# A Fourier mixer ahead of a feed-forward layer: units B multiply over 128 rows, with Y regrouped by SBUF-to-SBUF transfers

## The chip, the cores and the metric

The kernel runs on one core of a Trainium2 chip. The metric is the device time of one execution in microseconds (us), the lower the better. A core has five engines with a queue each: PE (the matrix engine; PEld is its loading of stationary operands), DVE (vector), ACT (activation), POOL (GpSimd) and SP, which in this kernel issues nearly all transfers.

## The reference

For each of 8 batches of 3008 positions by 256 channels, a Fourier transform is taken along the positions, each frequency is multiplied by a complex 256 by 256 matrix, soft-thresholded, and transformed back. All 24064 rows then go through a feed-forward layer with 2048 hidden channels.

```python
X = np.fft.rfft(x, axis=1)
Yr = Xr @ w_r - Xi @ w_i + b_r
Yi = Xr @ w_i + Xi @ w_r + b_i
Y  = sign(Y) * max(|Y| - 0.01, 0)            # Yr and Yi apart
y  = np.fft.irfft(Y, n=3008, axis=1)
h  = y.reshape(24064, 256) @ w_in
g  = where(h > 0, h, exp(min(h, 0)) - 1)
out = g @ w_out
```

## The kernel before

**The transform is cut into small units.** 3008 is 47 times 64, so each transform is made in two stages of matrix products with twiddle factors in the stationary operands. Per batch there are 6 units A (first stage, from the input tiles `xt0` to `xt2`, result to DRAM `DA`), 8 units X (second stage, from `Z`, which is loaded back from `DA`), 12 units M (the complex product, threshold and bias; two make one tile `Y` of 128 rows, 2 frequencies, 512 columns: real part in columns 0 to 255, imaginary part in 256 to 511), 6 units B (first stage back, result `Bz` to DRAM `DB`), and 8 units Y (second stage back, from `Bs`, loaded from `DB`; result `yT`).

**A unit B** (`unit_B`) takes one tile `Y` and multiplies it by `M3`. The rows of `Y` hold two groups `s` of 64 rows. The inverse stage sums over the 64 rows of a group and over the two parts `c`; so for each `(pp, s)` two matmuls of 64 rows are accumulated, one for each `c`. A unit is 8 matmuls of 64 rows by 256 columns, in pairs `s` = 0, 1 that lie on the lower and the upper 64 rows of the matrix engine. Its result of 1024 columns is moved to `Bz` by ACT, or by DVE in steps marked "act"; after every second unit SP stores `Bz` to `DB`. After B5, `load_Bs` brings everything back as `Bs` for the units Y.

**The feed-forward layer runs in 376 steps, 47 per batch.** A step handles 512 rows and 256 hidden channels: `front` makes 4 matmuls into `hps` and the exponential on ACT, `finish_elu` makes `gT` on DVE, and `back`, two steps later (`LAG`), makes 8 matmuls with `w_out_r` into `ps_o`. Every 8 steps `ps_o` is copied to `osb`, which has two buffers, and SP stores it to `out`.

**The order is written out by hand.** `plan(b)` lists for the 47 steps of batch b which unit of the next batch goes ahead of `front` (list `f0`) and what is issued behind it (list `f1`). A step is thus on PE: a unit, 4 matmuls `hps`, 8 matmuls `ps_o`. In steps marked "act" the elu is made by ACT and DVE without POOL, in steps marked "pool" by POOL too. Units M use POOL for three operations each (L301, L302, L303), the last of which writes `Y`. Each queue is in order, and a queue whose head waits holds all that is behind it.

**Tiles.** Pools with a tag have a fixed number of buffers. `Y` has 3 (`wk3`), `XS` (sums of the two parts for the units M) is a tile of its own, `M3` lies in the constant pool. Batch 0 has its own route (`split_B`, `turn_B`), which uses `M3` and `Y` directly; so the unit B of the change is used for batches 1 to 7, 42 times.

Of the kernel before, what the change touches and what calls it, by code (L numbers as in the profile page):

```python
# [8 lines left out]
ALU = mybir.AluOpType  # L9
# [11 lines left out]
N2 = 64  # L21
# [8 lines left out]
def kernel(  # L30
# [25 lines left out]
    constp = ctx.enter_context(tc.tile_pool(name="constp", bufs=1))  # L56
    M1 = constp.tile([P, P], F32R, name="M1")
    M2 = constp.tile([2 * NR, NS, 2, 2 * K1], BF16, name="M2")
    M3 = constp.tile([P, K1 // 2, 2, P], BF16, name="M3")
    M4 = constp.tile([4 * K1, 2 * N1], BF16, name="M4")  # L60
    wcat_r = constp.tile([P, 2, 2 * D], BF16, name="wcat_r")
    wcat_s = constp.tile([P, 2, 2 * D], BF16, name="wcat_s")
    w_in_s = constp.tile([P, 2, DFF], BF16, name="w_in_s")
    w_out_r = constp.tile([P, NFT, E], F32R, name="w_out_r")
    bias_bc = constp.tile([P, 2 * D], F32, name="bias_bc")
    bias_p = constp.tile([P, 2 * D], BF16, name="bias_p")
# [10 lines left out]
    space = constp.tile([P, 384], BF16, name="space")  # L77
# [24 lines left out]
    Z_of = {}  # L102
    XT_of = {}
    Y_of = {}
    Bz_of = {}
    DB_of = {}
    Bs_of = {}
# [119 lines left out]

    def sum_of(dt, ch):

        return XS[:, 3 * dt + ch] if 3 * dt + ch < 5 else busy[:]  # L230

    def three_weights(c, dt):

# [6 lines left out]
    def m_group(b, q, i, ps, biased=False):  # L240
        XT = XT_of[b]
        o = (2 * q + i) * P
        todo = [(c, dt) for c in range(2) for dt in range(2)]
        if b == 0:
            todo.sort(key=lambda z: z[1])
        for c, dt in todo:
            nc.tensor.matmul(  # L247
                ps, lhsT=XT[:, dt, c, o : o + P], rhs=(wcat_r, wcat_s)[c][:, dt, :],
                start=(not biased and (c, dt) == (0, 0)), stop=((c, dt) == (1, 1)),
            )  # L250
        if i == 0:
            Y_of[b, q] = wk3.tile([P, 2, 2 * D], BF16, name="Y", tag="Y")
        if biased:
            yb = ps
        else:
            yb = wk3.tile([P, 2 * D], F32, name="yb", tag="yb")[:]
            nc.vector.tensor_tensor(yb, ps, bias_bc[:], ALU.add)
        if (b, q, i) == (0, 2, 0):
            clip = late3.tile([P, 2 * D], F32, name="gT", tag="gT")
        else:  # L260
            clip = wk2.tile([P, 2 * D], F32, name="clip", tag="clip")
        return yb, clip

    def unit_M(b, q, i):
# [6 lines left out]
            return  # L271
        XT, o = XT_of[b], (2 * q + i) * P
        if i == 0:
            Y_of[b, q] = wk3.tile([P, 2, 2 * D], BF16, name="Y", tag="Y")
# [59 lines left out]
    def last_M(q, i):  # L334
# [26 lines left out]
        for Y_, yb, ch in todo:  # L361
            nc.vector.scalar_tensor_tensor(Y_, yb, LAM, ch, ALU.add, ALU.min)

    def unit_B(b, v, alone=False, on_dve=False, all_dve=False):
        if (b, v // 2) not in Bz_of:
            t = "A" if alone and v == 0 else "Bz"
            Bz_of[b, v // 2] = wk2.tile([P, 8, D], BF16, name=t, tag=t)
            if b not in DB_of:
                DB_of[b] = dram.tile([K1, P, D], BF16, name="DB", tag="DB")
        Bz, Y = Bz_of[b, v // 2], Y_of.pop((b, v))  # L370
        ps = unit_ps("bps", alone)
        for pp in range(2):
            for c in range(2):
                for s in range(2):
                    nc.tensor.matmul(  # L375
                        ps[:, s, pp * D : pp * D + D],
                        lhsT=M3[s * N2 : s * N2 + N2, 2 * v + pp, c, :],
                        rhs=Y[s * N2 : s * N2 + N2, pp, c * D : c * D + D],
                        start=(c == 0), stop=(c == 1),
                    )  # L380
        o = 4 * (v % 2)
        Bv = Bz[:, o : o + 4, :].rearrange("p (q s) d -> p s q d", s=2)
        psv = ps[:].rearrange("p s (q d) -> p s q d", d=D)
        if on_dve:
            nc.scalar.copy(Bv[:, :, 0], psv[:, :, 0])
            nc.vector.tensor_copy(Bv[:, :, 1], psv[:, :, 1])
        else:
            evac(Bv, psv, all_dve)
        if alone:
            k0 = 4 * v  # L390
            nc.sync.dma_start(
                DB_of[b][k0 : k0 + 4].rearrange("k p d -> p k d"), Bz[:, o : o + 4, :]
            )
        elif b == 1 and v > 3:
            nc.sync.dma_start(
                DB_of[b][4 * v : 4 * v + 4].rearrange("k p d -> p k d"), Bz[:, o : o + 4, :]
            )
        elif v % 2:
            k0 = 8 * (v // 2)
            nc.sync.dma_start(DB_of[b][k0 : k0 + 8].rearrange("k p d -> p k d"), Bz[:])  # L400
# [13 lines left out]
    def split_B(v, ps, on_dve=(False, True), by_half=False):  # L414
# [8 lines left out]
        def half(pp):  # L423
            for c in range(2):
                for s in range(2):
                    nc.tensor.matmul(
                        ps[s][:, pp * D : pp * D + D],
                        lhsT=M3[s * N2 : s * N2 + N2, 2 * v + pp, c, :],
                        rhs=Y[s * N2 : s * N2 + N2, pp, c * D : c * D + D],
                        start=(c == 0), stop=(c == 1),  # L430
                    )
# [22 lines left out]
    def turn_B(v, ts=(0, 1), ps=None, on_dve=False):  # L454
# [11 lines left out]
        for pp in range(2):  # L466
            for dt in ts:
                for c in range(2):
                    for s in range(2):
# [7 lines left out]
                            rhs=M3[s * N2 : s * N2 + N2, 2 * v + pp, c, :].rearrange(  # L477
                                "p (g m) -> p g m", g=4
                            )[:, :, 0:8],
                            start=(c == 0), stop=(c == 1),  # L480
# [69 lines left out]
    def idle_pe(n):  # L550

        for _ in range(n):
            nc.tensor.matmul(ips[:], lhsT=busy[:, 0:P], rhs=busy[:], start=True, stop=True)

    nc.vector.memset(bias_p[:], 0.0)
    bpd = dram.tile([3, 2 * D], BF16, name="bpd", tag="bpd")
    idle_pe(9)
# [272 lines left out]
    XS = sump.tile([P, 5, 512], BF16, name="XS")  # L830
# [60 lines left out]
    for o, src, sc, bi in ((1, w3, TURN, 0.0), (0, a3, -TURN, hpi[:])):  # L891
        if o == 0:
            nc.scalar.activation(a3[:], w3[:], AF.Abs)
        nc.scalar.activation(
            M3[:, :, 0, o * N2 : o * N2 + N2], src[:], AF.Sin, bias=bi, scale=sc
        )
    sgb = sg3[:].unsqueeze(2).to_broadcast([P, K1 // 2, N2])
    first_M(3, 0, True)
    nc.vector.scalar_tensor_tensor(
        M3[:, :, 1, 0:N2], M3[:, :, 0, N2:P], 2.0, sgb, ALU.mult, ALU.mult  # L900
    )
    nc.vector.scalar_tensor_tensor(
        M3[:, :, 1, N2:P], M3[:, :, 0, 0:N2], -2.0, sgb, ALU.mult, ALU.mult
    )
    first_M(3, 1, True)
    let_go()
# [203 lines left out]
    def plan(b):  # L1110
# [3 lines left out]
        mode = [None] * PER  # L1114
        n1, n2 = b + 1, b + 2
        mid = [("X", u) for u in range(8)] + [
# [4 lines left out]
        ]  # L1121
        if n1 < B:
            if b:
                lead, xs = 0, (3, 6, 9) if b < 3 else (3, 8, 13)

                def M(q):
                    return [("M", q, 0), ("M", q, 1)]
# [1 line left out]
                shift = b - 1 if b < 3 else b - 3  # L1129
                seq = [("y", 2), ("y", 3)] + [None] * shift + [("X", u) for u in range(8)]  # L1130
                if b < 3:
                    seq += [("y", 4)] + M(0) + M(1) + [("y", 5), ("B", 0)]
                else:
                    seq += M(0) + [("y", 4)] + M(1) + [("y", 5), ("B", 0)]
                seq += M(2) + [("y", 6), ("B", 1)] + M(3) + [("y", 7), ("B", 2)]
                on_act = [("X", 4), ("X", 7), ("B", 3)] + [("y", u) for u in range(5, 8)]
                if b < 3:
                    on_act += [("A", 0)]
                    seq += M(4) + [("B", 3)] + M(5) + [("A", 0), ("B", 4), ("B", 5)]
                    seq += [("A", u) for u in range(1, 6)]  # L1140
# [12 lines left out]
        else:  # L1153
            lead, seq = 0, [("y", u) for u in range(2, 8)]
        for t, u in enumerate(seq, lead):
# [26 lines left out]
        if b == 0:  # L1182
# [106 lines left out]
```

## Time and profile before

| | |
|---|---|
| runs without the profiler, median of 3 | 893.58 us (893.39 to 893.68) |
| span of the profiled execution, first to last instruction | 903.9 us |
| granted PE clock over the span | 0.948 |
| PE busy | 891.3 us, 99% of the span, 6917 matmuls |
| PEld / DVE / ACT / POOL busy | 675.2 / 679.6 / 722.4 / 596.7 us |
| matmuls of the units B (L375) | 336, in 42 units |
| transfers | 105.85 MB, mean 117 GB/s |

The span is the profiled execution's own time: nothing of the program lies around it in the page, and no other time of that execution is given. It is 10.3 us (1.2%) above the median of the runs without profiler. Busy times are unions of the instructions' intervals. A matmul's interval includes the time in which its result passes through the array, so matmuls that follow each other overlap; what one of them costs PE is read from the distance between two starts.

### The profile page before, as it was taken

Reading aid. Unit: us, or ns where it says so; the run is one execution under the profiler, and the core shown is the slowest. Engines: PE = TensorE matmul, PEld = TensorE weight load, DVE = VectorE, ACT = ScalarE, POOL = GpSimd, SP = SyncE. Lnnn points to the kernel's source line nnn. Section 1 sums busy time; section 2 is a strip of 40 time slices with the busy share of each in tenths; the row PEclk is TensorE's granted clock in tenths of the full one; section 3 lists DMA queues with packets and bytes.
Section 4 is the critical chain, followed back from the end, with each engine's and each line's share of the span. In section 5 each row is a group of like instructions: output and inputs, shape, how many; then the busy total and the mean of one; then the engine's idle time right before and its main releaser. Section 6 shows DMA issues by size and latency. Waiting matters only on the chain.

```text
span 903.9 us, 18292 instructions
## 1 busy us (share of the span) xinstructions
PE 891.3 (99%) x6917; PEld 675.2 (75%) x6917; DVE 679.6 (75%) x969; ACT 722.4 (80%) x1001; POOL 596.7 (66%) x806
## 2 busy tenths in 40 slices
PE   9999999999999999999999999999999999999997
PEld 3467667877788777877778777787777877777776
DVE  7788778688866887668866788677876678778776
ACT  6778778888978889798887988878887798776654
POOL 7562550788657886588756877559875697753664
PEclk9999999999999999999999999999999999999998
DMA  8996226631474115632265231643218201241111
GB/s 262 310 258 188 70 71 181 169 119 47 118 209 124 65 50 152 173 117 88 72 181 136 86 116 48 189 140 101 87 53 229 70 24 48 69 108 36 28 44 47
DMA packets 90718, 105.85 MB, mean 117 GB/s; under 512 B 5395, under 2 KB 81174, under 8 KB 87302
## 3 DMA queue, kind: packets, MB, share of 16 engines
q1 hardware_dynamic: 84278, 76.64, 30.0%
q0 software_dynamic: 5968, 27.26, 9.4%
q8 instruction: 54, 0.88, 0.4%
q10 hardware_dynamic: 384, 0.79, 0.3%
q14 instruction: 34, 0.28, 0.1%
HBM read 54.86 MB, written 49.81 MB: 116 GB/s over the span
## 4 chain that ended last, share of the span: by engine, by line
PE 90%; DVE 3%; DMA 3%; ACT 2%; POOL 1%; issue 1%; SPq 0%; DVEq 0%; ACTq 0%; POOLq 0%
PE ps_o L1080 37%; PE hps L1006 36%; PE mps L289 5%; PE bps L375 2%; PE xps L207 2%; PE yps L538 2%; PE aps L170 2%; DVE gT L1048 2%; PE mps L247 1%; DVE Bz L144 1%; DMA xt<-in_x_dram 1%; DMA Z<-DA 1%; DMA DB<-Bz 1%; PE sps L1006 1%; DMA DA<-A 0%
## 5 line engine op out<-in xcount | busy, mean ns | idle before, releaser
L1048 DVE SCALAR_TENSOR_TENSOR gT<-Et,hps 128x512 fp32r<-128x512 f32 (+1 forms) x544 | 423.7, 811 | 158.5 <-POOL Et L1059 115.4
L1080 PE MATMUL ps_o<-w_out_r,gT 128*128 128x256 f32 x3008 | 481.4, 303 | 0.0
L1080 PEld LDWEIGHTS ps_o<-w_out_r,gT 128*128 128x128 f32 x3008 | 407.7, 190 | 52.4 <-ACT osb L1092 0.5
L1059 POOL TENSOR_SCALAR Et<-Et 128x512 f32<-128x512 f32 x434 | 258.3, 614 | 223.6 <-ACT Et L1022 213.2
L1006 PE MATMUL hps<-yT,w_in_s 128*128 128x512 bf16 (+7 forms) x1688 | 388.9, 360 | 2.0 <-DVE gT L1048 1.3
L1022 ACT ACTIVATE Et<-hps 128x512 f32<-128x512 f32 x412 | 224.2, 598 | 67.8 <-PE hps L1006 63.3
L1006 PEld LDWEIGHTS <-w_in_s 128*128 128x128 bf16 x1728 | 144.7, 99 | 119.7 <-issue 21.7
L1024 ACT ACTIVATE Et<-hps 128x1024 f32<-128x1024 f32 x130 | 133.6, 1027 | 57.3 <-PE hps L1006 49.0
L1025 ACT ACTIVATE Et<-Et 128x1024 f32<-128x1024 f32 x130 | 137.4, 1057 | 4.1
L301 POOL TENSOR_TENSOR yb<-yb,bias_bc 128x512 f32<-128x512 f32 x72 | 92.3, 1282 | 9.5 <-DVE yb L296 9.4
L303 POOL TENSOR_TENSOR Y<-yb,clip 128x512 bf16<-128x512 f32 x72 | 92.6, 1286 | 6.0
L296 DVE TENSOR_TENSOR yb<-mps,yb 128x512 f32<-128x512 f32 x72 | 49.8, 692 | 7.6 <-PE hps L1006 0.5
L146 ACT CAST XT<-xps 128x768 bf16<-128x768 f32 x57 | 45.5, 799 | 9.8 <-PE xps L207 9.7
L146 ACT CAST A<-aps 128x1024 bf16<-128x1024 f32 x40 | 40.5, 1014 | 11.4 <-PE aps L170 9.9
L302 POOL TENSOR_SCALAR clip<-yb 128x512 f32<-128x512 f32 x72 | 44.2, 614 | 6.3
L289 PE MATMUL mps<-wcat_s,XT 128*128 128x256 bf16 x288 | 44.1, 277 | 0.0
L144 DVE COPY yb<-mps 128x256 f32<-128x256 f32 x72 | 30.3, 421 | 11.1 <-PE mps L289 9.7
L1050 DVE SCALAR_TENSOR_TENSOR gT<-hps,Et 128x1024 fp32r<-128x1024 f32 x29 | 35.5, 1223 | 2.4
L224 POOL TENSOR_TENSOR XS<-XT 128x512 bf16<-128x512 bf16 x30 | 34.1, 1159 | 2.1 <-ACT XT L146 1.2
L1092 DVE COPY osb<-ps_o 128x512 f32<-128x512 f32 x46 | 31.6, 686 | 1.2 <-PE ps_o L1080 0.5
L146 ACT CAST Bz<-bps 128x1024 bf16<-128x1024 f32 x32 | 31.9, 998 | 0.5 <-PE bps L375 0.4
L1027 ACT ACTIVATE Et<-hps 128x1024 f32<-128x1024 f32 x29 | 29.8, 1029 | 2.6 <-PE hps L1006 1.2
(184 smaller groups left out, 678.8 us busy)
## 6 DMA issues: line engine op xcount, KB each, us to landing
xt<-in_x_dram POOLq DMA_DIRECT2D x21, 1024.0 KB, 5.4
out_dram<-osb SPq DMA_DIRECT2D x158, 128.0 KB
Bs<-DB SPq DMA_DIRECT2D x30, 384.0 KB
DB<-Bz SPq DMA_DIRECT2D x20, 512.0 KB
DA<-A SPq DMA_DIRECT2D x19, 512.0 KB
Z<-DA SPq DMA_DIRECT2D x5, 1152.0 KB
Z<-DA SPq DMA_DIRECT2D x11, 384.0 KB
xt<-in_x_dram POOLq DMA_DIRECT2D x6, 512.0 KB, 6.0
```

Of the source, the lines that this page charges most:

```text
L146: nc.scalar.copy(dst, src)
L289: nc.tensor.matmul(out_, lhsT=lhs[:, dt] if lhs is not None else sum_of(dt, ch)[:, oc : oc + P], rhs=w[:, dt, :], start=(dt == 0), stop=(d ...
L296: nc.vector.tensor_tensor(yb[:].rearrange("p (c d) -> p c d", c=2), ps[:].rearrange("p (c d) -> p c d", c=2), yb[:, D : 2 * D].unsqueeze(1 ...
L301: nc.gpsimd.tensor_tensor(yb[:], yb[:], bias_bc[:], ALU.add)
L303: nc.gpsimd.tensor_tensor(Y_of[b, q][:, i, :], yb[:], clip[:], ALU.subtract)
L1006: nc.tensor.matmul(hps[s][:, c0:c1] if early else hps[:, s, c0:c1], lhsT=w_in_s[:, dt, ft * P : ft * P + P], rhs=yT_of[b][:, dt, t0 : t0 + ...
L1022: nc.scalar.activation(E_[:, s], hps[:, s], AF.Exp)
L1024: nc.scalar.activation(E_, hps[:], AF.Relu, scale=-1.0)
L1025: nc.scalar.activation(E_, E_, AF.Exp, scale=-1.0)
L1048: nc.vector.scalar_tensor_tensor(o, e, -1.0, h, ALU.add, ALU.max)
L1059: nc.gpsimd.tensor_scalar(E_[s], E_[s], 1.0, 0.0, ALU.min, ALU.max)
L1080: nc.tensor.matmul(po[q][:, i_ % 2, :], lhsT=gT[:, s, i_ * P : i_ * P + P], rhs=w_out_r[:, ft, :], start=(ft == 0 and i_ % 2 == 0), stop=( ...
```

## The change

Units B sum over 128 rows at once. For that the two parts `c` must lie one above the other in the partitions, for one group `s` at a time. A new tile `Yx` (128 rows: part 0 of a group in rows 0 to 63, part 1 in 64 to 127) is filled from `Y` by four transfers from SBUF to SBUF, each of 64 rows by 2 by 256 columns (64 KB), issued on SP (`turn_Y`). `M3` is regrouped once in the same way into `M3x` (`turn_M3`), by four transfers of 64 rows by 12 by 128 columns. A unit B is then 4 matmuls of 128 rows by 256 columns, none accumulated.

`turn_Y` stands in the step behind the second unit M of its tile, in `f1`, so on SP behind what the steps ahead have queued. `Y` and `Yx` share one tag with 4 buffers. To make room, `M3` becomes two tiles that borrow the buffers of `XS` and of one `osb` until `turn_M3` in step 6, `bias_p` borrows a buffer of `Bs`, and `space` shrinks.

The order moves too. For batches 2 to 7, B0 goes from ahead of the pair M2 to behind it and becomes an "act" step; B5 goes two units A further back; in `plan(1)` and `plan(2)` one empty step is put ahead of the units "n" (the first units Y of the next batch). For batch 1 (`plan(0)`), B0 to B3 go a pair of units M further back, A0 goes ahead of B4 and B5, which come one step later, and the first "n" is the third step behind B5 instead of the fourth. The loads of `x` in `plan(3)` to `plan(5)` are issued at steps 3, 6 and 9 instead of 3, 8 and 13.

```diff
-    M3 = constp.tile([P, K1 // 2, 2, P], BF16, name="M3")
+    M3x = constp.tile([P, K1 // 2, 2, P], BF16, name="M3x")
...
-            Y_of[b, q] = wk3.tile([P, 2, 2 * D], BF16, name="Y", tag="Y")
+            Y_of[b, q] = wk4.tile([P, 2, 2 * D], BF16, name="Y", tag="Y")
...
+    def by_part(dst, of):
+
+        for c in range(2):
+            for s in range(2):
+                nc.sync.dma_start(dst[c * N2 : c * N2 + N2, :, s, :], of(c, s))
+
+    def turn_M3():
+        by_part(M3x, lambda c, s: M3[c][s * N2 : s * N2 + N2])
+
+    def turn_Y(b, q):
+        Y = Y_of.pop((b, q))
+        Yx_of[b, q] = Yx = wk4.tile([P, 2, 2, D], BF16, name="Yx", tag="Y")
+        by_part(Yx, lambda c, s: Y[s * N2 : s * N2 + N2, :, c * D : c * D + D])
...
         for pp in range(2):
-            for c in range(2):
-                for s in range(2):
-                    nc.tensor.matmul(
-                        ps[:, s, pp * D : pp * D + D],
-                        lhsT=M3[s * N2 : s * N2 + N2, 2 * v + pp, c, :],
-                        rhs=Y[s * N2 : s * N2 + N2, pp, c * D : c * D + D],
-                        start=(c == 0), stop=(c == 1),
-                    )
+            for s in range(2):
+                nc.tensor.matmul(
+                    ps[:, s, pp * D : pp * D + D], lhsT=M3x[:, 2 * v + pp, s, :],
+                    rhs=Yx[:, pp, s, :], start=True, stop=True,
+                )
...
+    M3.append(sump.tile([P, K1 // 2, P], BF16, name="M3", tag="XS"))
+    M3.append(late2.tile([P, K1 // 2, P], BF16, name="M3", tag="osb"))
...
         mid = [("X", u) for u in range(8)] + [
-            ("M", 0, 0), ("M", 0, 1), ("M", 1, 0), ("M", 1, 1), ("B", 0), ("M", 2, 0),
-            ("M", 2, 1), ("B", 1), ("M", 3, 0), ("M", 3, 1), ("B", 2), ("M", 4, 0),
-            ("M", 4, 1), ("B", 3), ("M", 5, 0), ("M", 5, 1), ("B", 4),
-            ("A", 0), ("B", 5), ("A", 1), ("A", 2), ("A", 3), ("A", 4),
+            ("M", 0, 0), ("M", 0, 1), ("M", 1, 0), ("M", 1, 1), ("M", 2, 0), ("M", 2, 1),
+            ("B", 0), ("M", 3, 0), ("M", 3, 1), ("B", 1), ("M", 4, 0), ("M", 4, 1),
+            ("B", 2), ("M", 5, 0), ("M", 5, 1), ("B", 3), ("A", 0), ("B", 4), ("B", 5),
+            ("A", 1), ("A", 2), ("n", 0), ("n", 1), ("A", 3), ("A", 4), ("A", 5),
         ]
...
-                lead, xs = 0, (3, 6, 9) if b < 3 else (3, 8, 13)
+                lead, xs = 0, (3, 6, 9)
...
-                    seq += [("y", 4)] + M(0) + M(1) + [("y", 5), ("B", 0)]
+                    seq += [("y", 4)] + M(0) + M(1) + [("y", 5)] + M(2) + [("B", 0)]
                 else:
-                    seq += M(0) + [("y", 4)] + M(1) + [("y", 5), ("B", 0)]
-                seq += M(2) + [("y", 6), ("B", 1)] + M(3) + [("y", 7), ("B", 2)]
-                on_act = [("X", 4), ("X", 7), ("B", 3)] + [("y", u) for u in range(5, 8)]
+                    seq += M(0) + [("y", 4)] + M(1) + [("y", 5)] + M(2) + [("B", 0)]
+                seq += [("y", 6), ("B", 1)] + M(3) + [("y", 7), ("B", 2)]
+                on_act = [("X", 4), ("X", 7), ("B", 0), ("B", 3)] + [("y", u) for u in range(5, 8)]
                 if b < 3:
                     on_act += [("A", 0)]
-                    seq += M(4) + [("B", 3)] + M(5) + [("A", 0), ("B", 4), ("B", 5)]
-                    seq += [("A", u) for u in range(1, 6)]
+                    seq += M(4) + [("B", 3)] + M(5) + [("A", 0), ("B", 4), ("A", 1), ("A", 2)]
+                    seq += [("B", 5), ("A", 3), ("A", 4), ("A", 5), None]
                 else:
                     on_act += [("y", 4), ("B", 4)]
-                    seq += M(4) + [("B", 3), ("A", 0)] + M(5) + [("B", 4), ("A", 1), ("B", 5)]
-                    seq += [("A", u) for u in range(2, 6)] + [None] * (3 if n2 == B else 2)
+                    seq += M(4) + [("B", 3), ("A", 0)] + M(5) + [("B", 4)]
+                    seq += [("A", 1), ("A", 2), ("A", 3), ("B", 5), ("A", 4), ("A", 5)] + [None] * (3 if n2 == B else 2)
...
-                lead, seq = FILL, (
-                    [u for u in mid if u[0] != "A"]
-                    + [("A", 0), ("A", 1), ("A", 2), ("n", 0), ("n", 1)]
-                    + [("A", u) for u in range(3, 6)]
-                )
+                lead, seq = FILL, mid
...
+            if u[0] == "M" and u[2] == 1:
+                f1[t + 1].append((turn_Y, (n1, u[1])))
...
+            f1[6].append((turn_M3, ()))
```

More of the change, by code (lines that the diff above doesn't have):

```diff
@@ L65 @@
     bias_bc = constp.tile([P, 2 * D], F32, name="bias_bc")
-    bias_p = constp.tile([P, 2 * D], BF16, name="bias_p")
     lam_n = constp.tile([P, 1], F32, name="lam_n")
@@ L76 @@
     idm = constp.tile([P, P], BF16, name="idm")
-    space = constp.tile([P, 384], BF16, name="space")
+    space = constp.tile([P, 128], BF16, name="space")
     dram = ctx.enter_context(tc.tile_pool(name="dram", bufs=2, space=bass.MemoryType.DRAM))
@@ L104 @@
     Y_of = {}
+    Yx_of = {}
+    M3 = []
+    XS_of = []
     Bz_of = {}
@@ L228, in sum_of @@
     def sum_of(dt, ch):
-        return XS[:, 3 * dt + ch] if 3 * dt + ch < 5 else busy[:]
+        if 3 * dt + ch == 5:
+            return busy[:]
+        if not XS_of:
+            XS_of.append(sump.tile([P, 5, 512], BF16, name="XS", tag="XS"))
+        return XS_of[0][:, 3 * dt + ch]
     def three_weights(c, dt):
@@ L273, in unit_M @@
         if i == 0:
-            Y_of[b, q] = wk3.tile([P, 2, 2 * D], BF16, name="Y", tag="Y")
+            Y_of[b, q] = wk4.tile([P, 2, 2 * D], BF16, name="Y", tag="Y")
         ps, k1 = (
@@ L369, in unit_B @@
                 DB_of[b] = dram.tile([K1, P, D], BF16, name="DB", tag="DB")
-        Bz, Y = Bz_of[b, v // 2], Y_of.pop((b, v))
+        Bz, Yx = Bz_of[b, v // 2], Yx_of.pop((b, v))
         ps = unit_ps("bps", alone)
         for pp in range(2):
-            for c in range(2):
-                for s in range(2):
-                    nc.tensor.matmul(
-                        ps[:, s, pp * D : pp * D + D],
-                        lhsT=M3[s * N2 : s * N2 + N2, 2 * v + pp, c, :],
-                        rhs=Y[s * N2 : s * N2 + N2, pp, c * D : c * D + D],
-                        start=(c == 0), stop=(c == 1),
-                    )
+            for s in range(2):
[3 more added lines that the diff above has]
+                )
         o = 4 * (v % 2)
@@ L427, in half @@
                         ps[s][:, pp * D : pp * D + D],
-                        lhsT=M3[s * N2 : s * N2 + N2, 2 * v + pp, c, :],
+                        lhsT=M3[c][s * N2 : s * N2 + N2, 2 * v + pp, :],
                         rhs=Y[s * N2 : s * N2 + N2, pp, c * D : c * D + D],
@@ L476, in turn_B @@
                             ],
-                            rhs=M3[s * N2 : s * N2 + N2, 2 * v + pp, c, :].rearrange(
+                            rhs=M3[c][s * N2 : s * N2 + N2, 2 * v + pp, :].rearrange(
                                 "p (g m) -> p g m", g=4
@@ L553, in idle_pe @@
             nc.tensor.matmul(ips[:], lhsT=busy[:, 0:P], rhs=busy[:], start=True, stop=True)
+    bias_p = wk4.tile([P, 2 * D], BF16, name="bias_p", tag="Bs")
     nc.vector.memset(bias_p[:], 0.0)
@@ L829 @@
     sump = ctx.enter_context(tc.tile_pool(name="sump", bufs=1))
-    XS = sump.tile([P, 5, 512], BF16, name="XS")
+    M3.append(sump.tile([P, K1 // 2, P], BF16, name="M3", tag="XS"))
+    M3.append(late2.tile([P, K1 // 2, P], BF16, name="M3", tag="osb"))
     w_in_v = moe_w_in.rearrange("(c p) f -> p c f", p=P)
@@ L894 @@
         nc.scalar.activation(
-            M3[:, :, 0, o * N2 : o * N2 + N2], src[:], AF.Sin, bias=bi, scale=sc
+            M3[0][:, :, o * N2 : o * N2 + N2], src[:], AF.Sin, bias=bi, scale=sc
         )
@@ L899 @@
     nc.vector.scalar_tensor_tensor(
-        M3[:, :, 1, 0:N2], M3[:, :, 0, N2:P], 2.0, sgb, ALU.mult, ALU.mult
+        M3[1][:, :, 0:N2], M3[0][:, :, N2:P], 2.0, sgb, ALU.mult, ALU.mult
     )
     nc.vector.scalar_tensor_tensor(
-        M3[:, :, 1, N2:P], M3[:, :, 0, 0:N2], -2.0, sgb, ALU.mult, ALU.mult
+        M3[1][:, :, N2:P], M3[0][:, :, 0:N2], -2.0, sgb, ALU.mult, ALU.mult
     )
```

## The prediction

> **What bounds the kernel now.** I read the page's busy times and its chain first, then the groups of PE by form, then the timeline around two units B, and last SP's queue and its waits.
>
> ```profile
> PE 891.3 (99%) x6917; PEld 675.2 (75%) x6917; DVE 679.6 (75%) x969; ACT 722.4 (80%) x1001; POOL 596.7 (66%) x806
> PE 90%; DVE 3%; DMA 3%; ACT 2%; POOL 1%; issue 1%; SPq 0%; DVEq 0%; ACTq 0%; POOLq 0%
> ```
>
> PE never rests, and 90% of the chain that ended last is PE. The rows of PE in the view of waits add up to 6.7 us. So the kernel is as long as its PE work, and a nanosecond taken from PE comes off the end as long as no other engine or transfer becomes late.
>
> ```profile
> L289 PE MATMUL mps<-wcat_s,XT 128*128 128x256 bf16 x288 | 44.1, 277 | 0.0
> L375 PE MATMUL bps<-Y,M 64*128 64x256 bf16 x336 | 25.9, 274 | 0.2 <-ACT Bz L146 0.2
> ```
>
> Both rows have 256 columns, L289 over 128 rows, L375 over 64. A mean of 274 against 277 ns says that one matmul is as long either way. What counts is the distance of starts, which the timeline of batch 2 gives (start, duration, engine, line, count):
>
> ```profile
> 216.28 1.30 PE L1080 MATMUL ps_o<-w_out_r,gT 128*128 128x256 f32 x8
> 217.43 0.51 PE L538 MATMUL yps<-M,Bs 96*128 96x94 bf16 x8
> ...
> 218.48 1.30 PE L1080 MATMUL ps_o<-w_out_r,gT 128*128 128x256 f32 x8
> ...
> 219.51 1.28 POOL L303 TENSOR_TENSOR Y<-yb,clip 128x512 bf16<-128x512 f32 x1
> 219.71 0.62 PE L375 MATMUL bps<-Y,M 64*128 64x256 bf16 x8
> 220.26 1.07 PE L1006 MATMUL hps<-yT,w_in_s 128*128 128x512 bf16 x4
> 220.96 1.29 PE L1080 MATMUL ps_o<-w_out_r,gT 128*128 128x256 f32 x8
> 222.09 0.28 PE L289 MATMUL mps<-wcat_r,XS 128*128 128x256 bf16 x1
> ...
> 222.77 1.06 PE L1006 MATMUL hps<-yT,w_in_s 128*128 128x512 bf16 x4
> ...
> 227.22 0.62 PE L375 MATMUL bps<-Y,M 64*128 64x256 bf16 x8
> ```
>
> From `ps_o` to the unit behind it are 1.15 us (216.28 to 217.43, a unit Y) and 1.13 (220.96 to 222.09, a unit M), but 1.23 (218.48 to 219.71) for a unit B. The unit B itself takes 0.55 (219.71 to 220.26), a unit M of 6 matmuls 0.68 (222.09 to 222.77), so 0.114 each.
>
> **PE work: the term that decides.** By single starts, medians over all units: the last `ps_o` to the first `bps` is 211 ns, to the first `mps` 118. Inside a unit B the 8 matmuls start in pairs 2 to 4 ns apart, and the pairs 109 to 114 apart: the lower and upper half run side by side, so three pairs take 342 ns. The last pair to the first `hps` is 207 ns, while the last `mps` to `hps` is 114. So the halves already gain their factor of two; what the form costs is a gap of about 93 ns on the way in and 93 on the way out.
>
> After the change a unit is 4 matmuls of the L289 form: 4 x 114 = 456 instead of 549 ns, and 118 instead of 211 ahead of it. Saved: 93 + 93 = 186 ns a unit, 42 x 186 = 7.8 us of PE. The Trainium skill says the same in two rules (TensorEngine Tiling, "Key Properties" and "Theoretical Speedup"): a change of tiling mode drains the engine, and a contraction of 64 rows or fewer can run up to twice as fast by tiling. The second speaks against this change: by it alone the body gains nothing, which the 109 to 114 ns of a pair bear out; the gap of 93 ns at each end is the first.
>
> Bounds of this term: the body could be 4 x 118, and the gaps could stay in part where PE waits on the new transfers; from above, weight loads fall from 8 to 4 a unit, but they lie beside matmuls now. I take 7.8, range 6.5 to 8.2. The extra wait instruction of each unit on PE I take at nothing: 23 units A have one now, and the way from `ps_o` to them is 114 ns.
>
> **Four new transfers per tile on SP, and the wait for them.** A unit B now starts only when `Yx` has landed, so its old slack must hold a turn. The slack is the start of the unit less the end of the second Y on POOL: for B3 here 227.22 - (219.51 + 1.28) = 6.4 us. Over batches 2 to 7 the trace gives B1 7.0 to 8.3, B2 7.9 to 8.6, B3 6.2 to 6.4, B4 6.6 to 6.8, and B0 3.7 to 5.8, B5 1.5. Those two could not hold a turn, and they are the ones that move: B0 behind two steps M of 2.5 us (220.26 to 222.77), so over 8; B5 behind two steps A of 2.3, so 6.1. In batch 1 B0 to B3 gain two steps and B5 one, and none is under 5.5.
>
> What a turn takes, no row shows: there is no SBUF-to-SBUF transfer now. The nearest rows are the stores of `Bz`:
>
> ```profile
> 128.15 0.41 SPq L400 DMA_DIRECT2D DB<-Bz  x1
> ...
> 137.35 1.48 SPq L395 DMA_DIRECT2D DB<-Bz  x2
> 139.98 4.67 SPq L408 DMA_DIRECT2D Bs<-DB  x5
> ```
>
> An issue is 0.41 us, so the fourth starts 1.3 us after the first. The 256 KB store of 137.35 is done when the load at 139.98 may go: 2.6 us from issue, the fourth's likely bound, since it moves 64 KB. With 0.1 for the semaphore: 4.0 us from Y. The longest wait of a load for such a store is in SP's waits:
>
> ```profile
> SPq L408 <- DMA DB<-Bz: 22.9, 11, 4.4
> ```
>
> With 4.4 for the last transfer the turn is 5.8 us, still under B3's 6.2; from below, 2.5. I take 4.0, as the sizes are nearest to it, and 0 us of stall for all but one place. The Trainium skill (SBUF — State Buffer, "Door 1: The DMA port swizzle") says that partitions 0 to 63 reach only half of the ports. By it each of these transfers would move at half rate; the store of 128.15 alone shows 290 GB/s, so 0.45 instead of 0.23 us for 64 KB, a turn of 4.2.
>
> The place is B4 of batches 2 and 3. Its turn stands behind the stores of `out` and of B3's `Bz`:
>
> ```profile
> 229.92 1.56 SPq L1101 DMA_DIRECT2D out_dram<-osb  x2
> 231.58 10.10 SPq L400 DMA_DIRECT2D DB<-Bz  x2
> ```
>
> The turn can begin at 232.0 and lands at 236.0 to 237.8; B4 stands at 237.05, or 236.9 after the saving. So 0 to 0.9 us twice; I take 0.2 in all.
>
> Held behind a turn on SP are stores of `out` and `Bz`. A turn waits at the queue's head until Y ends, at most some 3 us, then issues for 1.8. `osb` comes back 8 steps (about 19 us) later; SP's 42 x 1.7 us = 71 us fit, as SP already stands waiting 10 us at a time (231.58 above). POOL's write of Y waits for an older turn, two tiles back, 7 us old or more. If that cover were gone POOL would be late by the difference, and the next unit B with it.
>
> **The order.** M0, M1 and M2 now follow with one step between. POOL needs 3.2 us a unit M (1.28 + 0.61 + 1.29) where a step is 2.5, and for batches 2 and 3 the sum into `XS` (1.16) too; Y of M2 then ends some 5 us behind the old distance to its matmuls at worst, but B2, its reader, stands seven steps later: covered. B0 as an "act" step gives DVE 1.22 + 1.22 = 2.4 us for a step of 2.3; behind two steps M of 2.3 in 2.5 that is no backlog. `back` reads `gT` two steps later. I take 0; bounds 0.3 x 6 = 1.8 us lost and 0.5 won, a part of the 1.9 us that PE waits for `gT` now (hps and sps rows).
>
> **B5 and "n" of batch 1.** B5 starts at 136.66 now and the first unit Y at 146.06, 9.4 later. One step (2.3) goes and 0.2 is saved: 6.9. B5's store is issued 1.8 after B5, done 2.6 to 4.4 later, the last load lands 2.1 to 2.6 after that: 6.5 to 8.8. Stall 0 to 1.9; I take 0.8. In batches 2 to 7 five steps (11.5 us) remain: covered.
>
> **At nothing:** `turn_M3` is issued where SP waits 4 us for the first `osb`; `M3x` is first read 30 us later. The first `osb` takes the buffer that a weight tile held; the second, 18 us later, the one of `M3`. The `x` loads at 3, 6, 9 are what batches 1 and 2 do now without a PE stall, and take 1 MB each out of the steps of units M, where the turns run; they have no reader until the units A.
>
> **Sum.** In the profiled execution 903.9 - 7.8 + 0.2 + 0.8 = 897.1 us, less 0.75%. The runs without profiler are 1.2% shorter than that span, so 6.7 of the 6.8 us are left there: 893.58 - 6.7 = **886.9 us**.
>
> **Rivals.**
> 1. *The gaps stay.* If the 93 ns belong to the wait for the PSUM buffer or the first weights of a unit, and not to the form, only the body counts, and 342 + 114 is what it is: gain near 0, 1 us of stalls, 894.4. Against it: all 42 units have the gap at both ends and no other kind of unit has it, whatever it waits for. 5%.
> 2. *Part is lost to turns behind busy queues:* B4 of two batches, "n" and DVE at their upper bounds, 1.8 + 1.9 + 1.8, with the low end of PE: 893.58 - 6.5 + 5.5 = 892.6 at the worst, 889.8 with half of that loss. For it: margins of 1 us. 20%.
> 3. *Yx comes late (slower).* If four transfers between SBUF partitions take 7.5 us from Y instead of 4.0, B3, B4 and B5 stall 1.3, 0.8 and 1.4 us in each of six batches: 21 us, less 7.8, 906.8. It beats the gain from about 6.8 us on (the stall of the three must reach 1.3 us a batch). By the half of the ports alone it does not get there. Against it: even the longest store gives 5.8. 14%.
>
> My forecast, 885.4 to 888.5, has 61%.
>
> **Numbers.** A measurement of this kernel can tell 0.2% (1.8 us). Range 884.9 to 891.8: below, 8.2 saved and 0.5 won by the order; above, most of rival 2. Outside lie rivals 1 and 3. Faster by over 0.2% 0.80, within 0.2% 0.06, slower 0.14.
>
> **What would show it.** Right: L375's successor has 168 matmuls of 128x256, 0.45 us from `bps` to `hps`, 1.14 from `ps_o` to `bps`; PE waits for DMA `Yx` near 0. Wrong: PE rows waiting for `Yx<-Y`, `bps` still 1.23 behind `ps_o`, SP's turns issued over 2 us after Y, or PE waiting for `Bs<-DB` at batch 1's "n".

## The result and the profile after

The changed kernel takes 896.29 us (median of 13 runs, 893.78 to 899.15), the kernel before beside it 893.98 us (13 runs, 893.39 to 895.41). The ratio is 1.0022, 95% interval 1.0012 to 1.0033: slower by 2.3 us, where 6.7 us less were forecast. The profiled execution has a span of 894.5 us at a granted PE clock of 1.000.

On the page of the kernel after, PE is no longer the whole of the chain: 83% where it was 90%, and transfers hold 4% where it was 3%.

```profile
PE 868.8 (97%) x6645; PEld 673.4 (75%) x6749; DVE 686.5 (77%) x969; ACT 723.2 (81%) x995; POOL 591.2 (66%) x794
PE 83%; DVE 6%; DMA 4%; ACT 2%; POOL 2%; issue 2%; SPq 1%; DVEq 0%; POOLq 0%
```

The new unit B stands in the groups of PE by form and in the timeline of batch 2 as foreseen: 168 matmuls of 128 rows, 1.12 us from `ps_o` to `bps` (222.99 to 224.11; it was 1.23), 0.44 from `bps` to `hps` (it was 0.55).

```profile
L295 PE MATMUL mps<-wcat_s,XT 128*128 128x256 bf16 x288 | 43.2, 273 | 0.0
L394 PE MATMUL bps<-Yx,M3x 128*128 128x256 bf16 x168 | 26.3, 275 | 0.8 <-DMA Yx<-Y 0.8
```

```profile
222.99 1.27 PE L1099 MATMUL ps_o<-w_out_r,gT 128*128 128x256 f32 x8
224.11 0.61 PE L394 MATMUL bps<-Yx,M3x 128*128 128x256 bf16 x4
224.55 1.03 PE L1025 MATMUL hps<-yT,w_in_s 128*128 128x512 bf16 x4
225.23 1.54 PE L1099 MATMUL ps_o<-w_out_r,gT 128*128 128x256 f32 x8
```

What is new is in PE's view of waits (us in total, times, longest): the units Y wait for `Bs`, and `hps` waits for `gT` 18 times instead of 3. (At the full clock the kernel before has 6 such waits, as its second profile below shows.)

```profile
PE yps L555 <- DMA Bs<-DB: 4.6, 3, 1.9
PE hps L1025 <- DVE gT L1067: 4.2, 18, 0.6
PE ips L570 <- DVE busy L564: 1.4, 1, 1.4
PE bps L394 <- DMA Yx<-Y: 0.8, 2, 0.4
```

By the distance of starts of PE, the three stalls at `Bs` are 2.1, 1.2 and 1.8 us, at the unit "n0" (the first unit Y) of batches 1, 2 and 3. The timeline shows where they come from. In batch 1:

```profile
130.32 0.38 SPq L417 DMA_DIRECT2D DB<-Bz  x1
130.93 2.91 SPq L374 DMA_DIRECT2D Yx<-Y  x4
...
133.39 1.04 ACT L148 CAST Bz<-bps 128x1024 bf16<-128x1024 f32 x1
133.88 2.53 SPq L1120 DMA_DIRECT2D out_dram<-osb  x4
...
136.52 1.14 SPq L412 DMA_DIRECT2D DB<-Bz  x2
139.12 2.97 SPq L425 DMA_DIRECT2D Bs<-DB  x5
...
144.08 0.49 PE L555 MATMUL yps<-M,Bs 96*128 96x94 bf16 x8 [1.93 <-DMA Bs<-DB]
```

SP never rests from 130.9 to 136.4: the turn (the four transfers of one tile) of `Y` for B5, and behind it four stores of `out`. The result of B4, in `Bz` at 134.4, is stored only at 136.5, and `Bs` goes out at 139.1. In batch 2 no turn stands near:

```profile
241.03 0.61 PE L394 MATMUL bps<-Yx,M3x 128*128 128x256 bf16 x4
...
242.72 0.36 SPq L417 DMA_DIRECT2D DB<-Bz  x1
243.74 2.55 SPq L1120 DMA_DIRECT2D out_dram<-osb  x4
246.38 0.55 SPq L187 DMA_DIRECT2D DA<-A  x1
247.02 2.70 SPq L425 DMA_DIRECT2D Bs<-DB  x4
```

The `Bs` loads are listed a step after B5, so they stand behind four stores of `out` and one of `DA`; and then the first of them needs 6.0 us to arrive. In the kernel before the same loads stood ahead of the four stores:

```profile
244.64 2.19 SPq L408 DMA_DIRECT2D Bs<-DB  x4
247.08 2.59 SPq L1101 DMA_DIRECT2D out_dram<-osb  x4
```

The chain of that stretch in the changed kernel (start, us, what) has the wait in one line:

```profile
246.38 0.55 SPq L187
...
247.02 6.02 DMA Bs<-DB
253.04 0.04 issue
253.08 0.51 PE yps L555 x8
```

The Trainium skill (DMA: Bandwidth & Descriptors, "Queues, rings and completion order") says that all transfers issued by SP go through the same rings and are consumed in ring order. The 6.0 us fit this: ahead of and among the loads lie 1 MB of stores and three more loads, and the DMA engines are 96% busy in that stretch.

### The profile page after: what moved, and what is told of

Its sections match the earlier page's. It is cut to its first block, busy times and chain, and to the rows that moved or that the text cites. A ratio compares the mean times of both kernels' runs of the same rounds, so it can differ in the third digit from the quotient of the medians.

```text
span 894.5 us, 18140 instructions
## 1 busy us (share of the span) xinstructions
PE 868.8 (97%) x6645; PEld 673.4 (75%) x6749; DVE 686.5 (77%) x969; ACT 723.2 (81%) x995; POOL 591.2 (66%) x794
## 4 chain that ended last, share of the span: by engine, by line
PE 83%; DVE 6%; DMA 4%; ACT 2%; POOL 2%; issue 2%; SPq 1%; DVEq 0%; POOLq 0%
PE ps_o L1099 35%; PE hps L1025 32%; PE mps L295 5%; DVE gT L1067 2%; PE xps L209 2%; PE bps L394 2%; PE yps L555 2%; DMA Bs<-DB 2%; DVE Bz L146 1%; PE mps L253 1%; PE aps L172 1%; PE sps L1025 1%; DMA Z<-DA 1%; DMA xt<-in_x_dram 1%; SPq L374 1%
## 5 line engine op out<-in xcount | busy, mean ns | idle before, releaser
L1078 POOL TENSOR_SCALAR Et<-Et 128x512 f32<-128x512 f32 x422 | 252.0, 616 | 227.0 <-ACT Et L1041 217.0
L1025 PE MATMUL hps<-yT,w_in_s 128*128 128x512 bf16 (+7 forms) x1594 | 370.6, 350 | 9.6 <-DVE gT L1067 4.2
L1041 ACT ACTIVATE Et<-hps 128x512 f32<-128x512 f32 x400 | 218.0, 599 | 63.5 <-PE hps L1025 59.6
L1043 ACT ACTIVATE Et<-hps 128x1024 f32<-128x1024 f32 x136 | 139.8, 1028 | 48.7 <-PE hps L1025 37.1
L1044 ACT ACTIVATE Et<-Et 128x1024 f32<-128x1024 f32 x136 | 143.8, 1057 | 4.3
L148 ACT CAST yT<-yps 128x752 bf16<-128x752 f32 x34 | 26.7, 786 | 11.2 <-PE yps L555 11.2
L555 PE MATMUL yps<-M,Bs 96*128 96x94 bf16 x448 | 28.5, 210 | 4.6 <-DMA Bs<-DB 4.6
```

The source lines that it names most:

```text
L148: nc.scalar.copy(dst, src)
L1025: nc.tensor.matmul(hps[s][:, c0:c1] if early else hps[:, s, c0:c1], lhsT=w_in_s[:, dt, ft * P : ft * P + P], rhs=yT_of[b][:, dt, t0 : t0 + ...
L1041: nc.scalar.activation(E_[:, s], hps[:, s], AF.Exp)
L1043: nc.scalar.activation(E_, hps[:], AF.Relu, scale=-1.0)
L1044: nc.scalar.activation(E_, E_, AF.Exp, scale=-1.0)
L1078: nc.gpsimd.tensor_scalar(E_[s], E_[s], 1.0, 0.0, ALU.min, ALU.max)
```

## The experiments

Two theories stood at the start. Theory 1: PE sets the end, the form is worth 7.8 us, and new stalls ate it. Theory 2: PE at its full clock is already held by the loop from `hps` over ACT and DVE back to PE, so that time taken from PE turns into waiting. All ratios are against the kernel before on the same chip. The start, up to the first `ps_o`, took 51.7 to 54.3 us in the traces without any order in it, so traces are compared from the first `ps_o` to the end: 834.7 us before, 837.3 after.

**The kernel before, once more.**

> The kernel before, unchanged, for a profile at the clock that its timed runs have (the profile that the prediction was read from had 0.948; the changed kernel's has 1.000). Theory 1 (PE sets the end at either clock; the saving is real and was eaten by new stalls): span about 892 us, `yps` to `hps` steps near the 42 ns of the first profile, PE's waits for `gT` as few as there (3 of 1.3 us in all), and the 64-row gaps still 93 ns in and out. Theory 2 (at full clock PE is already held by the loop hps -> ACT -> DVE -> hps, so that time taken from PE turns into waiting): `yps` to `hps` near the changed kernel's 140 ns, and waits for `gT` well above 1.3 us already before the change.

893.87 us, ratio 0.9999 (0.9990 to 1.0008). Its span is 891.4 us at a clock of 0.999, and the 12.5 us by which the first profile was longer go with its lower clock (`hps` steps 216 ns here, 224 there). `ps_o` to `bps` is 209 ns and `bps` to `hps` 202. `yps` to `hps` is 79 ns in the mean of 56 units, for 125 in the changed kernel (the median is 42 in both), and the waits for `gT` are 2.0 us: PE sets the end before the change, at this clock too. Theory 2 falls as a general statement. The 46 ns between the two means are 2.6 us in sum, and all of it lies in six units, y6 (the seventh unit Y) of batches 1 to 6; the run of the order alone comes back to them.

**The form alone.**

```diff
-            for c in range(2):
-                for s in range(2):
...
+            for s in range(2):
+                nc.tensor.matmul(
+                    ps[:, s, pp * D : pp * D + D], lhsT=M3[:, 2 * v + pp, s, :],
+                    rhs=Y[:, pp, s * D : s * D + D], start=True, stop=True,
+                )
```

> The kernel before with unit B alone in four matmuls over 128 rows, straight on Y and M3: no transfers, old order, old waits. The product of B is left incomplete (the 128-row sum mixes the two groups), the amount of work on every other engine is that of the kernel before. It prices the form alone. Theory 1: 42 units at 186 ns, so 7.8 us less, about 886 us. Theory 2: the gaps go (`bps` steps 109 ns, as in the changed kernel), but most of them comes back as waiting for `gT` or for the copies: 890.5 to 893.5 us.

889.46 us, ratio 0.9953 (0.9941 to 0.9965): 4.4 us less, between the two theories. Cut into steps (from one start of `ps_o` to the next), the 42 steps with a unit B are 7.1 us shorter in sum, and the other steps 2.8 us longer: 1.9 of it in the steps with units M, 0.7 in those with units A, and 2.3 of it in steps right behind a unit B. An example is B3 of batch 2. The kernel before in its second profile:

```profile
222.69 0.61 PE L375 MATMUL bps<-Y,M 64*128 64x256 bf16 x8
...
223.23 1.04 PE L1006 MATMUL hps<-yT,w_in_s 128*128 128x512 bf16 x4
...
223.89 0.57 ACT L1092 COPY osb<-ps_o 128x512 f32<-128x512 f32 x1
223.92 1.33 PE L1080 MATMUL ps_o<-w_out_r,gT 128*128 128x256 f32 x8
...
225.09 0.28 PE L289 MATMUL mps<-wcat_r,XS 128*128 128x256 bf16 x1
```

The form alone:

```profile
221.95 0.61 PE L374 MATMUL bps<-Y,M 128*128 128x256 bf16 x4
...
222.39 1.03 PE L1003 MATMUL hps<-yT,w_in_s 128*128 128x512 bf16 x4
...
223.07 1.54 PE L1077 MATMUL ps_o<-w_out_r,gT 128*128 128x256 f32 x8
223.25 0.57 ACT L1089 COPY osb<-ps_o 128x512 f32<-128x512 f32 x1
...
223.87 0.55 PEld L1077 LDWEIGHTS ps_o<-w_out_r,gT 128*128 128x128 f32 x4 [0.17 <-ACT osb L1089]
...
224.45 0.28 PE L289 MATMUL mps<-wcat_r,XS 128*128 128x256 bf16 x1
```

From `bps` to `ps_o` the step is 0.11 shorter (1.12 for 1.23), but from there to `mps` it is 0.21 longer (1.38 for 1.17): the second half of `ps_o` needs the bank that ACT copies to `osb`. The copy began 0.03 us ahead of `ps_o` before, and 0.18 behind it now. PE ran ahead of ACT, and waits. In other steps the wait is for `gT`: 3.5 us instead of 2.0. Theory 2 holds there, step by step.

**The order alone.** The changed `plan`, units B over 64 rows as before.

```diff
-                    seq += M(4) + [("B", 3)] + M(5) + [("A", 0), ("B", 4), ("B", 5)]
-                    seq += [("A", u) for u in range(1, 6)]
+                    seq += M(4) + [("B", 3)] + M(5) + [("A", 0), ("B", 4), ("A", 1), ("A", 2)]
+                    seq += [("B", 5), ("A", 3), ("A", 4), ("A", 5), None]
```

> The kernel before with the changed order and x steps alone: B units over 64 rows as before, no transfers, no Yx. Theory 1a (B5's later place is what makes Bs late at the n units of batches 1 to 3): the n stalls of 5.1 us in sum stay, the whole 3 to 5 us slower than before, 897 to 899 us. Theory 1b (the transfers' issues on SP make Bs late): n stalls under 1 us each batch, within 1 us of before. Theory 2: as 1a for the stalls at n; elsewhere nothing.

897.23 us, ratio 1.0041 (1.0030 to 1.0053): 3.4 us slower without one transfer. PE waits for `Bs` at "n0" of batches 1 to 3 for 0.6, 0.8 and 1.6 us, 3.0 in sum; before, none of the three waits. So 1a for batches 2 and 3, and 1b for batch 1, where the changed kernel has 2.1.

```profile
PE yps L538 <- DMA Bs<-DB: 2.5, 3, 1.4
PE hps L1006 <- DVE gT L1048: 2.5, 11, 0.6
```

Cut into steps, this run has a second loss, which none of the theories has: the step of y6 is 0.34 us longer in each of six batches, 2.0 us in sum (0.44 and 2.6 us in the changed kernel); the other steps are 1.2 us shorter. y6 now stands right behind B0. The kernel before in its second profile, where y6 stands behind M2:

```profile
202.26 1.21 DVE L1048 SCALAR_TENSOR_TENSOR gT<-Et,hps 128x1024 fp32r<-128x1024 f32 x1
203.17 0.51 PE L538 MATMUL yps<-M,Bs 96*128 96x94 bf16 x8
203.53 1.02 PE L1006 MATMUL hps<-yT,w_in_s 128*128 128x512 bf16 x3
```

The order alone:

```profile
201.59 1.23 DVE L144 CAST Bz<-bps 128x1024 bf16<-128x1024 f32 x1 [0.35 <-PE bps L375]
202.74 1.21 DVE L1048 SCALAR_TENSOR_TENSOR gT<-Et,hps 128x1024 fp32r<-128x1024 f32 x1
203.28 0.51 PE L538 MATMUL yps<-M,Bs 96*128 96x94 bf16 x8
204.00 1.02 PE L1006 MATMUL hps<-yT,w_in_s 128*128 128x512 bf16 x3 [0.21 <-DVE gT L1048]
```

In B0's "act" step DVE moves `Bz` first and then makes `gT` of the step before, which reads a tile `hps`. `hps` has two buffers, so the matmuls of the next step need the one that `gT` reads: `gT` ends at 203.95 and they start at 204.00, 0.72 us behind `yps` for 0.36 before. No run takes B0's "act" step back alone; the cause is read from these lines.

**`Bs` loaded early, from old data.**

```diff
...
-            if u == ("B", 5):
-                f1[t + (b > 0 and n2 < B)] += [
-                    (load_Bs, (n1, w, 0, 4 * K1 - 16 * (b == w == 0))) for w in range(4)
-                ]
+            if u == ("B", 3):
+                f1[t] += [(load_Bs, (n1, w, 0, 4 * K1, b)) for w in range(4)]
```

> The changed kernel with the Bs loads issued behind B3 and reading the DB of the batch before, so that nothing at n waits for them (Y of a batch is then made from old data; all sizes and counts are the same). Theory 1: the 5.1 us of stalls at n go, about 891 us, faster than before by 2.5 to 3. Theory 2: part of the 5.1 us comes back as other waits, 893 to 895 us, no faster than before.

896.75 us, ratio 1.0033 (1.0021 to 1.0045). That is above what either theory expected. The stalls at "n" are gone and nothing is won: the four loads now stand ahead of a turn on SP, and B5 waits for `Yx` 2.5 us in batch 2 and 1.6 in batch 3. It doesn't show what the "n" stalls are worth; it shows that a place in SP's queue is taken from another.

```profile
PE bps L394 <- DMA Yx<-Y: 4.6, 4, 2.4
PE hps L1025 <- DVE gT L1067: 4.4, 19, 0.6
```

This gave theory 3: the price of the transfers is SP's queue, through the issues of the turns and through what stands behind what. Three runs price the transfers, in the changed order throughout.

**No transfers.** `turn_Y` is not issued, and B multiplies `Y`.

```diff
-            if u[0] == "M" and u[2] == 1:
-                f1[t + 1].append((turn_Y, (n1, u[1])))
...
-                    rhs=Yx[:, pp, s, :], start=True, stop=True,
+                    rhs=Y[:, pp, s * D : s * D + D], start=True, stop=True,
```

> The changed kernel without any transfer: B multiplies 128 rows of Y itself, in the changed order (B's product mixes the two groups). If form and order add up as they were measured apart (-4.4 and +3.4 us), 892.9 us; the n stall of batch 1 under 0.7 us, those of batches 2 and 3 as in the run of the order alone (2 us in sum). If the form's gain depends on the order, up to 2 us off this.

892.94 us, ratio 0.9985 (0.9974 to 0.9996). Form and order add up: -1.2 us by the medians, where -4.4 and +3.4 give -1.0. The stalls at "n0" are 0.7, 0.6 and 1.6 us, as in the order alone.

**Transfers that nobody reads.**

```diff
...
-                    rhs=Yx[:, pp, s, :], start=True, stop=True,
+                    rhs=w_in_s[:, pp, s * D : s * D + D], start=True, stop=True,
```

> The changed kernel with unit B multiplying constant data (w_in_s) in place of Yx: the four transfers per tile are issued as before, but nothing on PE waits for them (B's product is left out of the result). What it adds to the run without transfers is the price of the transfers' issues and bytes. Theory 3 (one queue: 0.6 us per issue on SP push out stores, DB stores and Bs loads back): about 895.5 us, the changed kernel's 896.3 less the waits for Yx of some 0.8 us, with the n stall of batch 1 at 2 us. Rival (the waits for Yx are the price): as the run without transfers, 893.

896.69 us, ratio 1.0016 (1.0001 to 1.0031), as slow as the changed kernel. So the waits for `Yx` cost less than these runs can tell. By steps, those with a unit B are 1.0 us longer in the changed kernel's trace than in this one. The rest of the turns' price doesn't hang on their reader: "n0" of batch 1 waits 2.9 us, for 0.7 without them.

**One transfer of the same bytes.**

```diff
-        by_part(Yx, lambda c, s: Y[s * N2 : s * N2 + N2, :, c * D : c * D + D])
+        nc.sync.dma_start(Yx[:].rearrange("p a s d -> p a (s d)"), Y[:])
...
```

> The changed kernel with B multiplying constant data, and each tile's four transfers replaced by one of the same bytes (a plain copy of Y to Yx, read by nobody). Against the run with four unread transfers (896.7 us) it tells the issues from the bytes. Theory 3 (issues of 0.6 us on SP): near the run without transfers, 893 us. Rival (the bytes): 896 us.

894.04 us, ratio 1.0002 (0.9990 to 1.0013). It lies between the two, and its interval meets both. In the one trace, "n0" of batch 1 waits 0.5 us, and from the first `ps_o` to the end are 833.8 us, as without transfers (833.8; with four unread, 837.9). That points to the issues, but one trace is not the runs: how the price divides between issues and bytes is not settled.

The other runs move work between or along the queues.

**Turns issued by POOL.**

```diff
-                nc.sync.dma_start(dst[c * N2 : c * N2 + N2, :, s, :], of(c, s))
+                eng.dma_start(dst[c * N2 : c * N2 + N2, :, s, :], of(c, s))
```

> The changed kernel with the transfers of Y issued by GpSimd's queue in place of SP's; the result is the reference's. Theory 3: SP's queue is as short as before the change, the n stall of batch 1 falls from 2.1 to about 0.6 us and the waits for Yx stay small: 893.5 to 895 us. Rival: 24 issues of 0.59 us (as the x loads take on this queue) in each batch's M steps, on the engine that also makes Y and elu's part, make Y and gT late: 899 us or more.

947.92 us, ratio 1.0588 (1.0564 to 1.0611): the rival. POOL spends 102 us on the issues, 2.4 us at a time in the steps of units M, and `Et`, `gT` and PE stand behind them. PE's waits for `gT` are 37.4 us. The Trainium skill (Perfetto Trace Analysis, "DMA Optimizations") says that spreading the issues over the engines may help where making descriptors is the bottleneck; here it costs 51.6 us over the changed kernel, where the turns as a whole cost 3.4, since that engine is in the loop that feeds PE.

```profile
L374 POOL DMA_DIRECT2D Yx<-Y x168 | 102.4, 613 | 13.2 <-POOL Y L309 10.0 <-issue 1.9 <-POOL Y L276 1.2
```

**B5 a step earlier.**

```diff
-                    seq += M(4) + [("B", 3)] + M(5) + [("A", 0), ("B", 4), ("A", 1), ("A", 2)]
-                    seq += [("B", 5), ("A", 3), ("A", 4), ("A", 5), None]
+                    seq += M(4) + [("B", 3)] + M(5) + [("A", 0), ("B", 4), ("A", 1), ("B", 5)]
+                    seq += [("A", 2), ("A", 3), ("A", 4), ("A", 5), None]
```

> The changed kernel with B5 of batches 2 and 3 one step earlier (B4, A1, B5, A2 in place of B4, A1, A2, B5); the result is the reference's. Theory 3: the n stalls of these two batches (1.2 and 1.8 us) go, 893.3 to 894 us. Rival: with a step (2.2 us) less for Y5's transfers, B5 waits for Yx instead, up to 2 us in each batch, 895 to 897 us.

896.45 us, ratio 1.0018 (1.0003 to 1.0033), as the changed kernel. Both sides are half right: "n0" of batches 2 and 3 no longer waits, and B5 of batch 2 waits 1.6 us for `Yx`. There the second `Y` of M5 is ready only 6 us after its matmuls, as POOL is behind.

**`Bs` issued in B5's own step.**

```diff
-                f1[t + (b > 0 and n2 < B)] += [
+                f1[t] += [
```

> The changed kernel with the second of these moves alone: Bs loads of batches 2 to 7 issued in B5's own step. The result is the reference's. Theory 3: the stalls at n of batches 2 and 3 (1.2 and 1.8 us) go, that of batch 1 stays, 893.5 to 894.5 us. Rival: SP then waits for the DB store at the head of its queue, and out stores and DA stores behind it come late: no gain, 896.

894.99 us, ratio 1.0003 (0.9993 to 1.0012). The time is 0.5 us above what was expected. In the trace no "n0" of batches 2 and 3 waits; that of batch 1 waits 1.3 us. In batch 2 the loads go out 4.9 us behind B5 instead of 6.0, and that is enough: the loss there is gone by one place in a queue.

**Early issue: this, and each turn ahead of the next step's unit.**

```diff
-                f1[t + 1].append((turn_Y, (n1, u[1])))
+                f0[t + 1].append((turn_Y, (n1, u[1])))
```

> The changed kernel with two moves on SP's queue alone: each tile's four transfers are issued before the unit of the following step (so they no longer stand behind a DB store that waits for Bz), and the Bs loads of batches 2 to 7 are issued in B5's own step, ahead of out stores and DA store. PE, DVE, ACT and POOL keep their order; the result is the reference's. Theory 3 (the price of the change is SP's queue: 0.6 us per issue, and waits at its head): n stalls of batches 1 to 3 fall from 5.1 to under 2 us and the Yx waits go, 892 to 893.5 us. Rival (the bytes in the rings make them late): unchanged, 895.5 to 897.

891.62 us, ratio 0.9974 (0.9963 to 0.9984): faster than both kernels, as theory 3 had it (its expected 892 to 893.5 was a little high). No instruction of PE, DVE, ACT or POOL changed its order. In the profiled execution, one of its slower ones at 894.45 us, "n0" of batch 1 still waits 2.1 us.

**The first of the four `Bs` loads ahead of the others.**

```diff
-                f1[t] += [
-                    (load_Bs, (n1, w, 0, 4 * K1 - 16 * (b == w == 0))) for w in range(4)
-                ]
+                f1[t].append((load_Bs, (n1, 0, 0, 4 * K1 - 16 * (b == 0))))
+                f1[t + (int(n2 < B) if b else 4)] += [(load_Bs, (n1, w)) for w in range(1, 4)]
```

> The run with early issue on SP (891.6 us), and in addition the first of the four Bs loads of a batch (w0, the only one that the n units read) issued alone in B5's step, the other three 4 steps later in batch 1 and one step later in batches 2 to 6 (batch 7: in the same step). The result is the reference's. Theory 3, carried on: what is left at n in batch 1 (1.9 us in that run's profile) is w0 sharing the rings with w1 to w3; it falls under 1 us, 890 to 891.5 us. Rival: w0 is late because DB's store lands late, or the later three come too late for y of the next batch: 891.6 us or more.

891.88 us, ratio 0.9964 (0.9953 to 0.9976); from the run before it this can't be told apart, and it is above the 890 to 891.5 that theory 3 expected. Its profile has what was sought in batch 1: two issues of `Bs` are enough, and "n0" stalls 0.4 us. That this stall is gone in one trace and the time no shorter leaves open what it was worth in the run before.

```profile
129.14 2.54 SPq L374 DMA_DIRECT2D Yx<-Y  x4
...
135.55 1.44 SPq L412 DMA_DIRECT2D DB<-Bz  x2
...
138.16 1.19 SPq L425 DMA_DIRECT2D Bs<-DB  x2
...
142.22 0.49 PE L555 MATMUL yps<-M,Bs 96*128 96x94 bf16 x8 [0.23 <-ACT Et L1046]
```

## Why the prediction was wrong, step by step

**PE work: half right.** The gaps belong to the form and went: 209 to 121 ns on the way in, 202 to 109 on the way out (the kernel before against the form alone), as the 93 ns read from the trace had it; rival 1 is refuted. These numbers fit the rule that the prediction cites from the Trainium skill (TensorEngine Tiling, "Key Properties"), that a change of tiling mode drains the engine. The steps with a unit B got 7.1 us shorter, for 7.8. What failed is the sentence under the chain: "a nanosecond taken from PE comes off the end as long as no other engine or transfer becomes late". Other engines were late at once, by 0.1 to 0.2 us, mostly in the steps right behind a unit B, and 2.8 us came back as waits. Alone, the term measured 4.4 us. The 6.7 us of PE's waits in the first profile spoke for PE, but a wait that is absent says nothing of how near it is; the distance from the end of `gT` or of the `osb` copy to its reader on PE, step by step, would have.

**"In batches 2 to 7 five steps (11.5 us) remain: covered."** This step failed for batches 2 and 3, which stall by 1.2 and 1.8 us. For batch 1 the prediction had worked out 6.5 to 8.8 us from B5 to the last load; for the others it set 11.5 us against that sum, but there the loads go out a step later, behind four stores of `out` and one of `DA`. Measured in batch 2: 6.0 us from B5 (241.03) to the issue (247.02) and 6.0 more to arrival, 12.0 us, where 10.9 were there ("n0" was due at 251.9).

**"`back` reads `gT` two steps later. I take 0"** for B0 as an "act" step. `back` was not the nearest reader to ask about. `gT` holds the tile `hps` that the next step's matmuls need, and this step, that of y6, is 0.34 us longer in six batches in the order alone and 0.44 in the changed kernel: 2.0 and 2.6 us, where 1.8 was the bound.

**B5 and "n" of batch 1: 0.8 us taken, 2.1 found**, just beyond the upper bound of 1.9. By parts, in the changed kernel's trace: B5's store is issued 2.1 us behind B5, for the 1.8 set; the load that waits for it goes out 3.2 later, within the 2.6 to 4.4; from there to "n0" are 3.7, for the 2.1 to 2.6 set. In the run without transfers the three are 1.7, 2.4 and 3.6. So the load's time was set too short, with or without the turn. The turn adds 1.2 us at the store: B5's goes out 0.6 us behind B4's instead of 2.3, as the turn and the stores of `out` had held B4's back.

**Turns on SP.** An issue takes 0.61 us in the median, not 0.41, so a turn holds SP 2.5 to 2.9 us instead of 1.7. Still the waits for `Yx` are small: between their first two matmuls B4 of batch 3 and B5 of batch 7 stall 0.5 and 0.6 us, for 0.2 taken in all. Rival 3, by which the kernel would be slower because `Yx` comes late, is refuted; the kernel was slower by other ways. The turns cost more by what waits behind them than by what waits for them.

**The order, taken at 0** with bounds of -0.5 and +1.8: alone it costs 3.4 us (3.8 in the traces: 3.0 at "n0" and 2.0 at y6, less 1.2 elsewhere).

**The sum.** From 886.9 to 896.3 are 9.4 us. The changed kernel's trace against the second of the kernel before has the same 9.4 (2.6 us longer, for 6.8 less): 3.0 at "n0" of batches 2 and 3, 1.3 at that of batch 1, 2.6 at y6, 2.1 handed back in the steps with units M and A, 0.8 at the steps with a unit B (the waits for `Yx`), less 0.4 in the others. These are single traces, so a few tenths of each may be chance. Rival 2 had two of the mechanisms, turns behind busy queues and DVE in B0's step, but its worst case ended at 892.6, since "n" had a price in one batch only and nothing was to be handed back. What was put at nothing at the start can't be judged: its 0.5 us are within the spread of that stretch.

## What to carry to other kernels

Where one queue carries all transfers, price a new issue by what stands behind it and by the next deadline of that, not by the wait of its own reader; and for a step that is moved, follow its load to the place where it is issued, with all that lies ahead of it. For work that is moved to another engine, ask for the nearest reader of what stands behind it there, a buffer that has to come free included. A gain on the bounding engine is worth only what the other engines can follow: look for the steps in which they end within a tenth of a microsecond of being late. If a change fails by a queue, try the order of issue before giving up the change: here two such moves turned +2.3 us into -2.9, with the 2.6 us at y6 still in the kernel.

## What was not expected of the hardware

The issue of a 64 KB transfer from 64 partitions to 64 others holds SP for 0.61 us in the median and up to 1.56, a 512 KB store of `Bz` to DRAM only 0.39. The granted PE clock of one kernel was 0.948 in one profiled execution and 0.999 in another, 12.5 us of span apart. And in the five traces in which a tile is turned by four transfers on SP and the `Bs` loads go out together behind B5, "n0" of batch 1 waited 2.1, 2.9, 1.1, 1.3 and 2.1 us for much the same queue. In four of them the second load goes out 5.3 to 5.5 us behind B5, and in the one with early turns 4.1; but from there to "n0" pass 2.8 to 4.8 us. The timed runs of these kernels spread over 3 to 6 us, those of the kernel before over 2 to 5. What varies there is not settled.
